# Row maxima transposed unclipped, with VectorE clipping, negating and flagging the transposed rows out of PSUM

## The chip, the cores and the metric

The kernel runs on one core of one Trainium2 chip. The metric is the device time of one execution in microseconds. Of the kernel before there are three timed runs, with a median of 907.64 us (907.53 to 913.1), and one profiled execution of 907.15 us, from which all rows below come.

## The reference, cut to what matters

Attention over 2 batches x 8 heads, 768 tokens, head size 64, in which a query sees only the keys whose nearest centroid (of 16) is its own; behind it two feed-forward networks on the 1536 x 512 result. What the change touches is the row maximum of the masked scores:

```python
scores = scale * np.matmul(q, k.transpose(0, 1, 3, 2))
scores = np.where(mask, scores, -1000000000.0)
scores = scores - np.max(scores, axis=-1, keepdims=True)
attn = np.exp(scores)
attn = attn / (np.sum(attn, axis=-1, keepdims=True) + 1e-09)
return np.matmul(attn, v).astype(np.float32)
```

A query whose cluster holds no key at all has every score at the same huge negative value. Its attention is then the mean of V, and the kernel treats it apart by a flag per query.

## The kernel before, in words

**Work and stages.** The 16 heads are taken as 8 pairs (`NP`). Behind a lead-in that fills the pipeline come 8 steps, `step(0)` to `step(7)`, then the two feed-forward networks. In step j three pairs are in work at once: pair j has its scores (`st`), exponentials (`et`) and products with V (`av`); pair j+1 (called m) has its row maxima; pair j+2 (p) has its transposes (`tp`), its products with the centroids (`dt`, `ds`) and its mask rows. POOL adds up the exponentials of a head over its key tiles (`ea`).

**Row maxima of pair m.** `maxes` (L278) computes for 128 queries and half the keys the masked scores again in PSUM (`mxs`, L283), and VectorE reduces each to a maximum (L289): 24 per step, kept in `mx`, 128 x 24. At the end of the step `max_rows1` (L293) reduces the two halves to one maximum per query and head, `mf`, 128 x 12 (L298). It then writes three blocks of 12 columns into `nm`: the maximum clipped from below and negated (L299), and twice the flag "no key" (L301). `max_rows2` (L304) transposes the 128 x 36 block on TensorE (`nt`, L309), ScalarE copies the rows into SBUF (`nr`, L311), and two moves that SP issues (both recorded at L138) carry them to where the next step's matmuls read them: row 80 of `QT` (read by every second score matmul, L352) and four flag rows of `GR` (read by the first matmul of `av`, L375, and by the sums, L397).

**What sets the order.** Each engine runs its instructions in the order in which they were written, and waits in place. The table `P` gives every piece of a step a position; the pieces are sorted by it. `max_rows1` stands at 21.65 and `max_rows2` at 26.91, so between the two stand, on TensorE, one or two matmul groups of `av` and nothing else. Behind the transpose on TensorE come the rest of `av`, the small V sum (`vt`, L327), the transposes of the next pair (`tp`, L164) and the first scores of the next step. SP carries all the moves and loads, in order. PSUM tiles that are named by `bank` rotate over six banks.

In the lead-in `max_rows1(0)` and `max_rows2(0)` run once, at a time at which POOL has no work. So there are eight of these transposes: one in the lead-in, seven at the ends of steps 0 to 6.

Of the kernel before, what the change touches and what calls it, by code (L numbers as in the profile page):

```python
# [10 lines left out]
F32 = mybir.dt.float32  # L11
F32R = mybir.dt.float32r
# [3 lines left out]
ALU = mybir.AluOpType  # L16
AX = mybir.AxisListType
BIG = float(2.0 ** 100)
CLIP = float(2.0 ** 60)
# [8 lines left out]
def clustered_attention_two_ffns(  # L28
# [20 lines left out]
    nc = tc.nc  # L49
    B, H, S, D = q.shape  # L50
    C = cent.shape[1]
    DM = out.shape[1]
    KF = w1.shape[0]
    NT = S // 128
# [10 lines left out]
    def bank(nm):  # L65
        nbank[0] += 1
        return ps1.tile([128, 512], F32, tag=f"s{nbank[0] % 6}", name=nm)
# [3 lines left out]
    ident = const.tile([128, 128], F32, name="ident")  # L71
# [14 lines left out]
    ap_ = att.enter_context(tc.tile_pool(name="att", bufs=1))  # L86
    et_p = att.enter_context(tc.tile_pool(name="et", bufs=6))
    ea_p = att.enter_context(tc.tile_pool(name="ea", bufs=2))
    nm_p = att.enter_context(tc.tile_pool(name="nmp", bufs=1))
# [4 lines left out]
    def slots(n, nm):  # L94
        last = (NP - 1) % n
        return [(ap_ if s == last else er2).tile([128, 2, 2, S], F32R, name=f"{nm}{s}") for s in range(n)]


    QT = slots(3, "qt")
# [7 lines left out]
    gv = ap_.tile([128, 128], F32R, name="gv")  # L107
    GR = [gr[64 * s:64 * s + 4] for s in range(2)]
    GV = [gv[64 * s:64 * s + 4] for s in range(2)]

    ok = set()
    qraw, kraw = {}, {}
# [24 lines left out]
    def move(dst, src):  # L137
        nc.sync.dma_start(out=dst.bitcast(F32), in_=src.bitcast(F32))  # L138
# [137 lines left out]
    nm_t = {}  # L276
# [11 lines left out]
            ok.add(("mx", j))  # L288
        nc.vector.tensor_reduce(out=nm_t[j][:, h, i, n:n + 1], in_=t[:, 0:HS], axis=AX.X, op=ALU.max)  # L289

    nr_t = {}

    def max_rows1(j):  # L293
        m = nm_t.pop(j)
        assert ("mx", j) in ok
        nm = nm_p.tile([128, 3, 2 * NT], F32, tag="nm", name="nm", bufs=2)
        mf = nm_p.tile([128, 2 * NT], F32, tag="mf", name="mf", bufs=2)
        nc.vector.tensor_reduce(out=mf, in_=m.rearrange("p h i n -> p (h i) n"), axis=AX.X, op=ALU.max)  # L298
        nc.vector.tensor_scalar(nm[:, 0, :], mf, -CLIP, -1.0, op0=ALU.max, op1=ALU.mult)  # L299
        for x in (1, 2):  # L300
            nc.vector.tensor_scalar(nm[:, x, :], mf, -CLIP, None, op0=ALU.is_le)  # L301
        nr_t[j] = nm

    def max_rows2(j):  # L304
        nm = nr_t.pop(j)
        assert j < 2 or ("sm", j - 2) in ok
        ok.add(("mr", j))
        t = bank("nt")
        nc.tensor.transpose(t[0:36, 0:128], nm.rearrange("p a b -> p (a b)"), ident)  # L309
        nr = nm_p.tile([36, 128], F32R, tag="nr", name="nr", bufs=2)  # L310
        nc.scalar.copy(nr, t[0:36, 0:128])  # L311
        move(QT[j % 3][64 + C:65 + C, 1, :, :], nr[0:12, :])
        move(GR[j % 2], nr[12:36, :])

    vs_t = {}

# [8 lines left out]
    def vsum2(j):  # L325
# [5 lines left out]
        tl = nm_p.tile([2, 128], F32R, tag="tl", name="tl")  # L331
        g = GV[j % 2]

# [34 lines left out]
    def av(j, kt, n):  # L368
# [4 lines left out]
        if kt == 0:  # L373
            assert ("gv", j) in ok
            nc.tensor.matmul(t[:, 0:HS], lhsT=GV[j % 2], rhs=GR[j % 2][:, r], start=True, stop=False)  # L375
        for h in range(2):
# [232 lines left out]
    with tc.manual_schedule():  # L609
# [27 lines left out]
        nc.gpsimd.memset(g768.bitcast(F32), 0.0)  # L637
        nc.gpsimd.memset(gr.bitcast(F32), 0.0)
        nc.gpsimd.memset(gv.bitcast(F32), 0.0)

# [7 lines left out]
        for _ in range(2):  # L650
            nc.vector.reciprocal(ss[:, 2:3], ss[:, 1:2])
            nc.vector.scalar_tensor_tensor(
                out=ss[:, 1:2], in0=ss[:, 2:3], scalar=ss[:, 0:1], in1=ss[:, 1:2], op0=ALU.mult, op1=ALU.add
# [26 lines left out]
        def step(j):  # L680
# [21 lines left out]
            put(at["V1"], lambda: vsum1(m), m is not None)  # L702
            put(at["V2"], lambda: vsum2(m), m is not None)
            put(at["MR"][0], lambda: max_rows1(m), m is not None)
            put(at["MR"][1], lambda: max_rows2(m), m is not None)
            put(at["LK"], lambda: late_k(m), m is not None)
            put(at["LD"], lambda: load(p + 1), p is not None and p + 1 < NP)
# [12 lines left out]
        lead += [(le["MV"][w], lambda w=w: moves(1, "qk"[w])) for w in range(2)]  # L720
        lead += [(le["V1"], lambda: vsum1(0)), (le["V2"], lambda: vsum2(0))]
        lead += [(le["MR"][0], lambda: max_rows1(0)), (le["MR"][1], lambda: max_rows2(0))]
        lead += [(le["MX"][x], lambda x=x: maxes(0, x)) for x in range(4 * NT)]
        for j in range(3):
# [24 lines left out]
        for c, fn in ((KF - 1, evac_av), (KF - 2, evac_sums)):  # L749
            t = pools["wb"].tile([128, 2 * NW], F32R, tag=f"w{c}", name="last").bitcast(F32)  # L750
# [79 lines left out]
```

## Time and profile before

| what | value |
|---|---|
| median of 3 runs | 907.64 us |
| profiled execution | 907.15 us |
| its span, first to last instruction | 905.4 us |
| PE busy | 838.6 us (93%) |
| DVE busy | 645.0 us (71%) |
| ACT busy | 442.0 us (49%) |
| POOL busy | 168.3 us (19%) |
| attention (lead-in and steps 0 to 7) | up to about 340 us |
| mean granted TensorE clock | 0.962 of full speed |

The span is what lies between the first and the last instruction; 1.75 us of the execution lie outside it. The steps repeat nearly to the microsecond: the maxima of step 4 are reduced at 221.56 us, those of step 5 at 259.34 us. So one step read closely stands for the others. Step 7 has no maxima of its own, and step 6 has no transposes of a next pair.

### The profile page before, as it was taken

The numbers are of one execution on the slowest core, as the hardware profiler recorded it, in microseconds if no ns is written. First come the engines' busy times: TensorE is split into PE (matmuls) and PEld (weight loads), VectorE is DVE, ScalarE is ACT, GpSimd is POOL, SyncE is SP. The second block draws the span as 40 slices with busy tenths as digits, with TensorE's granted clock in tenths as the row PEclk, the third lists the DMA queues.
The fourth block names the chain that finished last, engine by engine and source line by source line (L and its number), as shares of the span: only waits on it lengthen the run. The fifth ranks groups of instructions, "written<-read, shape, count | busy, mean of one in ns | idle before, by whom it ended". The sixth has DMA issues, their size and how long they took to land.

```text
span 905.4 us, 10141 instructions
## 1 busy us (share of the span) xinstructions
PE 838.6 (93%) x3721; PEld 612.2 (68%) x3721; DVE 645.0 (71%) x955; ACT 442.0 (49%) x772; POOL 168.3 (19%) x110
## 2 busy tenths in 40 slices
PE   6698898988989967999999999999899999999997
PEld 6565465654645425777888888876678878887885
DVE  6776877868768586887201137887999888888886
ACT  3145354553545534334322233335667776776764
POOL 2063745738458320000000000000000000000000
PEclk9598999999999979999999999999899999999999
DMA  9776364563620729000000005552000010001001
GB/s 195 172 162 146 62 140 89 116 145 77 141 54 12 303 86 401 0 1 1 1 0 1 1 23 209 186 186 93 1 1 1 0 47 1 1 0 47 1 1 47
DMA packets 44290, 71.37 MB, mean 79 GB/s; under 512 B 28320, under 2 KB 30672, under 8 KB 40144
## 3 DMA queue, kind: packets, MB, share of 16 engines
q1 hardware_dynamic: 44240, 70.72, 27.8%
q8 instruction: 29, 0.48, 0.2%
q14 instruction: 21, 0.17, 0.1%
HBM read 43.03 MB, written 3.15 MB: 51 GB/s over the span
## 4 chain that ended last, share of the span: by engine, by line
PE 57%; DVE 28%; ACT 10%; issue 3%; DMA 2%; SPq 0%; DVEq 0%; ACTq 0%
PE av L377 7%; PE h L513 6%; PE h L514 6%; PE h L515 6%; DVE w L474 4%; DVE w L480 4%; PE yp L589 4%; PE yp L590 4%; PE st L351 4%; PE yp L588 4%; PE mxs L283 3%; ACT w L484 3%; PE st L352 3%; DVE w L468 2%; PE yp L585 2%
## 5 line engine op out<-in xcount | busy, mean ns | idle before, releaser
L513 PE MATMUL h<-xh,w 128*128 128x512 f32 x384 | 151.1, 393 | 2.9 <-ACT last L410 2.9
L514 PE MATMUL h<-xl,w 128*128 128x512 f32 x384 | 150.9, 393 | 0.0
L515 PE MATMUL h<-xh,w 128*128 128x512 f32 x384 | 150.8, 393 | 0.0
L356 ACT ACTIVATE et<-st 128x384 f32<-128x384 f32 x192 | 88.6, 488 | 69.3 <-PE st L352 66.0
L289 DVE TENSOR_REDUCE mx<-mxs 128x1 f32<-128x384 f32 x192 | 98.1, 551 | 29.6 <-PE mxs L283 29.5
L362 POOL TENSOR_TENSOR ea<-ea,et 128x768 f32<-128x768 f32 x60 | 109.5, 1844 | 30.7 <-ACT et L356 30.7
L569 DVE TENSOR_TENSOR gl<-y,gh 128x512 fp32r<-128x512 f32 x48 | 33.2, 692 | 96.1 <-ACT gh L561 96.1
L377 PE MATMUL av<-et,vr 128*64 128x384 f32 x384 | 94.0, 565 | 5.8 <-ACT et L356 5.7
L484 ACT CAST w<-w 128x1024 fp32r<-128x1024 f32 x32 | 33.6, 1049 | 124.5 <-DVE w L480 124.5
L513 PEld LDWEIGHTS h<-xh,w 128*128 128x128 f32 x384 | 72.2, 188 | 20.0 <-ACT last L410 3.6
L515 PEld LDWEIGHTS h<-xh,w 128*128 128x128 f32 x384 | 72.2, 188 | 16.5
L514 PEld LDWEIGHTS h<-xl,w 128*128 128x128 f32 x384 | 72.2, 188 | 16.4
L588 PE MATMUL yp<-w,gh 128*128 128x512 f32 x192 | 76.9, 400 | 6.5 <-ACT gh L563 6.3
L585 PE MATMUL yp<-gl,w 128*128 128x512 f32 x192 | 77.6, 404 | 4.1 <-DVE gl L569 4.1
L584 PE MATMUL yp<-gh,w 128*128 128x512 f32 x192 | 76.8, 400 | 3.8 <-ACT gh L561 3.8
L589 PE MATMUL yp<-w,gl 128*128 128x512 f32 x192 | 77.5, 404 | 2.0 <-DVE gl L571 1.9
L590 PE MATMUL yp<-w,gh 128*128 128x512 f32 x192 | 76.3, 397 | 0.0
L586 PE MATMUL yp<-gh,w 128*128 128x512 f32 x192 | 75.5, 393 | 0.0
L351 PE MATMUL st<-qt,kk 128*128 128x384 f32 x192 | 73.6, 383 | 0.0
L526 ACT ACTIVATE y<-h 128x512 f32<-128x512 f32 x48 | 28.5, 594 | 81.9 <-PE h L515 81.8
L283 PE MATMUL mxs<-kt,qt 80*128 80x384 f32 x192 | 63.0, 386 | 5.6 <-DMA kt<-mr 5.6
L352 PE MATMUL st<-qt,kt 81*128 81x384 f32 x192 | 65.9, 343 | 0.0
(140 smaller groups left out, 1452.2 us busy)
## 6 DMA issues: line engine op xcount, KB each, us to landing
w<-in_moe_w SPq DMA_DIRECT2D x32, 1024.0 KB
qt<-hiq SPq DMA_DIRECT2D x16, 384.0 KB
kk<-hik SPq DMA_DIRECT2D x32, 192.0 KB
qraw<-in_q SPq DMA_DIRECT2D x8, 384.0 KB
kraw<-in_k SPq DMA_DIRECT2D x8, 384.0 KB
vr<-in_v SPq DMA_DIRECT2D x8, 384.0 KB
qt<-loq SPq DMA_DIRECT2D x16, 192.0 KB
kt<-hik SPq DMA_DIRECT2D x16, 192.0 KB
```

What stands on the lines that cost most here:

```text
L289: nc.vector.tensor_reduce(out=nm_t[j][:, h, i, n:n + 1], in_=t[:, 0:HS], axis=AX.X, op=ALU.max)
L351: nc.tensor.matmul(t[:, 0:HS], lhsT=KK[j % 2][:, h, c], rhs=QT[j % 3][:, 0, h, r], start=True, stop=False)
L352: nc.tensor.matmul(t[:, 0:HS], lhsT=KT[j % 3][0:65 + C, 1, h, c], rhs=QT[j % 3][0:65 + C, 1, h, r], start=False, stop=True)
L362: eng.tensor_tensor(out=ea[j, h], in0=et[j, 0, h] if first else ea[j, h], in1=e, op=ALU.add)
L377: nc.tensor.matmul(t[64 * h:64 * h + 64, 0:HS], lhsT=VR[j % 2][:, h, kt, :], rhs=et[j, kt, h][:, n, :], start=False, stop=kt == NT - 1,)
L513: nc.tensor.matmul(t, lhsT=wh[:, kk, :], rhs=h, start=kk == 0, stop=False)
L514: nc.tensor.matmul(t, lhsT=wh[:, kk, :], rhs=l, start=False, stop=False)
L515: nc.tensor.matmul(t, lhsT=wl[:, kk, :], rhs=h, start=False, stop=kk == KD - 1)
L585: nc.tensor.matmul(t, lhsT=wh[:, s], rhs=gl, start=False, stop=False)
L588: nc.tensor.matmul(t, lhsT=gh[:, s], rhs=wh, start=first, stop=False)
L589: nc.tensor.matmul(t, lhsT=gl[:, s], rhs=wh, start=False, stop=False)
L590: nc.tensor.matmul(t, lhsT=gh[:, s], rhs=wl, start=False, stop=last)
```

## The change

`max_rows1` now only reduces, and writes the unclipped maxima twice, 32 columns apart, into a tile `MF` that is zeroed once by POOL. `max_rows2` transposes 44 columns of that (12 maxima, 20 zeros, 12 maxima again). In place of ScalarE's copy, VectorE reads the transposed rows in PSUM: rows 0 to 11 are clipped and negated, rows 32 to 43 become flags, both written to `nr`. The flag rows go to `GR` by two moves of two rows each, where one move of four rows did it before.

```diff
+    MF = [ap_.tile([128, 2, 32], F32, name=f"mf{s}") for s in range(2)]
...
     def max_rows1(j):
-        m = nm_t.pop(j)
+        m = nm_t.pop(j).rearrange("p h i n -> p (h i) n")
         assert ("mx", j) in ok
-        nm = nm_p.tile([128, 3, 2 * NT], F32, tag="nm", name="nm", bufs=2)
-        mf = nm_p.tile([128, 2 * NT], F32, tag="mf", name="mf", bufs=2)
-        nc.vector.tensor_reduce(out=mf, in_=m.rearrange("p h i n -> p (h i) n"), axis=AX.X, op=ALU.max)
-        nc.vector.tensor_scalar(nm[:, 0, :], mf, -CLIP, -1.0, op0=ALU.max, op1=ALU.mult)
-        for x in (1, 2):
-            nc.vector.tensor_scalar(nm[:, x, :], mf, -CLIP, None, op0=ALU.is_le)
-        nr_t[j] = nm
+        nc.vector.tensor_reduce(
+            out=MF[j % 2][:, :, 0:2 * NT], in_=m.unsqueeze(1).to_broadcast([128, 2, 2 * NT, 2]), axis=AX.X, op=ALU.max
+        )
 
     def max_rows2(j):
-        nm = nr_t.pop(j)
...
-        nc.tensor.transpose(t[0:36, 0:128], nm.rearrange("p a b -> p (a b)"), ident)
-        nr = nm_p.tile([36, 128], F32R, tag="nr", name="nr", bufs=2)
-        nc.scalar.copy(nr, t[0:36, 0:128])
-        move(QT[j % 3][64 + C:65 + C, 1, :, :], nr[0:12, :])
-        move(GR[j % 2], nr[12:36, :])
+        w = 32 + 2 * NT
+        nc.tensor.transpose(t[0:w, 0:128], MF[j % 2].rearrange("p a b -> p (a b)")[:, 0:w], ident)
+        nr = nm_p.tile([w, 128], F32R, tag="nr", name="nr", bufs=2)
+        nc.vector.tensor_scalar(nr[0:2 * NT, :], t[0:2 * NT, 0:128], -CLIP, -1.0, op0=ALU.max, op1=ALU.mult)
+        nc.vector.tensor_scalar(nr[32:w, :], t[32:w, 0:128], -CLIP, None, op0=ALU.is_le)
+        move(QT[j % 3][64 + C:65 + C, 1, :, :], nr[0:2 * NT, :])
+        for x in range(2):
+            move(GR[j % 2][2 * x:2 * x + 2], nr[32:w, :])
...
+        for s in range(2):
+            nc.gpsimd.memset(MF[s], 0.0)
```

On VectorE, at the end of step 3, the order before was this (`mx` are the maxima, `t`, `gv` and `tl` the V sum, `loq` the next pair's queries):

```order
L289 TENSOR_REDUCE mx<-mxs 128x1 x13
L298 TENSOR_REDUCE mf<-mx 128x12
L299 TENSOR_SCALAR nm<-mf 128x12
L301 TENSOR_SCALAR nm<-mf 128x12 x2
L335 TENSOR_TENSOR t_1897<-vt,bm 2x128
```

It is now this, with line numbers of the changed kernel:

```order
L291 TENSOR_REDUCE mx<-mxs 128x1 x13
L297 TENSOR_REDUCE mf_112<-mx 128x2x12
L308 TENSOR_SCALAR nr<-nt 12x128
L309 TENSOR_SCALAR nr<-nt 12x128
L334 TENSOR_TENSOR t_1886<-vt,bm 2x128
```

Three small operations ahead of the transpose have become two behind it; all others keep their places. On TensorE the same place reads in the changed kernel as below; only the transposed width (36 before, 44 now) differs.

```order
L376 MATMUL av<-et,vr_109 64x384 x2
L306 MATMUL nt<-ident,mf_112 44x128
L376 MATMUL av<-et,vr_109 64x384 x2
L326 MATMUL vt<-vs,ones 2x128
L166 MATMUL tp<-ident,qraw 128x128 x6
L376 MATMUL av<-et,vr_109 64x384 x4
L166 MATMUL tp<-ident,kraw 128x128 x3
L350 MATMUL st<-qt_101,kk_106 128x384
```

On SP's queue the changed kernel has, at the same place, one move more:

```order
L130 DMA kraw<-in_k 128x12x64
L140 DMA qt_101<-nr 1x12x128
L140 DMA gr<-nr 2x6x128 x2
L140 DMA gv<-tl 2x128
L140 DMA qt_100<-hiq 64x2x768
```

Everything behind the `gr` moves stands one issue later than before. The copy of `nr` leaves ScalarE, eight times.

## Rows read from the trace of the kernel before

**Rows 1.** Waits of the whole span: engine, line, releaser: total us, times, longest us.

```profile
PE nt L309 <- DVE nm L301: 21.2, 8, 2.7
```

**Rows 2.** Instructions that write `nm`: durations in ns, first and last start in us.

```profile
L301 DVE TENSOR_SCALAR nm<-mf x16: 158/168/1773, 40.5 to 293.8; 128x12 f32<-128x12 f32 x16
```

**Rows 3.** Timeline of the end of step 4: start us, us, engine, line, instruction.

```profile
221.42 3.57 POOL L362 TENSOR_TENSOR ea<-ea,et 128x768 f32<-128x768 f32 x2 [1.21 <-ACT et L356]
...
221.56 0.87 PE L377 MATMUL av<-et,vr 128*64 128x384 f32 x4
221.56 0.18 DVE L298 TENSOR_REDUCE mf<-mx 128x12 f32<-128x24 f32 x1
221.77 1.48 DVE L299 TENSOR_SCALAR nm<-mf 128x12 f32<-128x12 f32 x1
223.17 1.85 DVE L301 TENSOR_SCALAR nm<-mf 128x12 f32<-128x12 f32 x2
...
225.07 0.29 PE L309 MATMUL nt<-ident,nm 128*36 128x128 f32 x1 [2.65 <-DVE nm L301]
...
225.29 1.37 PE L377 MATMUL av<-et,vr 128*64 128x384 f32 x4
...
225.68 0.86 SPq L138 DMA_DIRECT2D qt<-nr  x1
...
226.59 0.59 PE L327 MATMUL vt<-vs,ones 128*2 128x128 f32 x2
226.59 0.68 SPq L138 DMA_DIRECT2D gr<-nr  x1
...
227.11 1.54 PE L164 MATMUL tp<-ident,qraw 128*128 128x128 f32 x6
227.21 0.28 DVE L335 TENSOR_TENSOR t<-vt,bm 2x128 f32<-2x128 f32 x1 [2.20 <-PE vt L327]
...
228.57 1.20 DVE L176 SCALAR_TENSOR_TENSOR loq<-tp,hiq 128x384 fp32r<-128x384 f32 x2 [0.26 <-ACT hiq L173]
...
228.58 1.66 PE L377 MATMUL av<-et,vr 128*64 128x384 f32 x8
...
230.17 0.55 PE L164 MATMUL tp<-ident,kraw 128*128 128x128 f32 x3
...
230.47 0.42 PE L351 MATMUL st<-qt,kk 128*128 128x384 f32 x1
...
230.74 0.34 PE L352 MATMUL st<-qt,kt 81*128 81x384 f32 x1
...
234.46 0.43 PE L375 MATMUL av<-gr,gv 4*128 4x384 f32 x1
```

**Rows 4.** Timeline of the lead-in behind its transpose.

```profile
41.47 0.85 SPq L138 DMA_DIRECT2D qt<-nr  x1
...
43.83 0.52 PE L352 MATMUL st<-qt,kt 81*128 81x384 f32 x1
```

**Rows 5.** Stretches behind the seven waits: us, PE busy, granted clock, DMA share, GB/s.

```profile
72.25:79.10 6.85, 6.85 (x24) 0.53 0.18 37
111.52:117.02 5.50, 5.50 (x25) 0.69 0.17 37
...
225.07:230.47 5.40, 5.40 (x24) 0.68 0.01 4
262.84:267.18 4.34, 4.34 (x16) 0.61 0.02 4
295.61:300.79 5.18, 5.18 (x20) 0.67 0.16 32
```

**Rows 6.** Other stretches: us, then PE, PEld, DVE, ACT, POOL busy, clock, DMA share.

```profile
222.40:225.00 2.60, 0.02 (x2) 0.00 (x0) 2.60 (x3) 0.00 (x0) 2.59 (x2) 1.00 0.06 10
193.50:221.50 28.00, 27.16 (x145) 17.45 (x143) 23.27 (x39) 15.51 (x34) 18.23 (x12) 1.00 0.63 140
320.00:324.00 4.00, 1.48 (x4) 0.57 (x4) 2.89 (x3) 2.58 (x5) 1.07 (x1) 0.64 0.16 68
```

More of the change, by code (lines that the diff above doesn't have):

```diff
@@ L289, in maxes @@
         nc.vector.tensor_reduce(out=nm_t[j][:, h, i, n:n + 1], in_=t[:, 0:HS], axis=AX.X, op=ALU.max)
-    nr_t = {}
     def max_rows1(j):
-        m = nm_t.pop(j)
+        m = nm_t.pop(j).rearrange("p h i n -> p (h i) n")
         assert ("mx", j) in ok
-        nm = nm_p.tile([128, 3, 2 * NT], F32, tag="nm", name="nm", bufs=2)
-        mf = nm_p.tile([128, 2 * NT], F32, tag="mf", name="mf", bufs=2)
-        nc.vector.tensor_reduce(out=mf, in_=m.rearrange("p h i n -> p (h i) n"), axis=AX.X, op=ALU.max)
-        nc.vector.tensor_scalar(nm[:, 0, :], mf, -CLIP, -1.0, op0=ALU.max, op1=ALU.mult)
-        for x in (1, 2):
-            nc.vector.tensor_scalar(nm[:, x, :], mf, -CLIP, None, op0=ALU.is_le)
-        nr_t[j] = nm
+        nc.vector.tensor_reduce(
+            out=MF[j % 2][:, :, 0:2 * NT], in_=m.unsqueeze(1).to_broadcast([128, 2, 2 * NT, 2]), axis=AX.X, op=ALU.max
+        )
     def max_rows2(j):
-        nm = nr_t.pop(j)
         assert j < 2 or ("sm", j - 2) in ok
```

## The prediction

> **What bounds the kernel now.** I began with the list of waits, which adds up for each engine what it stood still for. TensorE is the busiest engine, so its waits are what can be won. Its largest is at the transpose of the row maxima, which waits for VectorE's small operations: 21.2 us in 8 waits [rows 1]. The longest, 2.7 us, is that of the lead-in; the other seven are 2.65 us each, 18.5 us together.
>
> Next, the durations of the operations waited for. The flag operation on 128x12 numbers takes 158 ns at the least and 1773 ns at the most [rows 2]: the same work, eleven times as long. The timeline of one step's end shows when [rows 3]. POOL runs two additions from 221.42 to 224.99, so one ends at about 223.2. VectorE's first small operation starts at 221.77 and lasts until 223.25; the next starts at 223.17, is drawn out to the end of POOL's second addition, and the third follows in no time. The reduction ahead of them, next to the same addition, took 0.18. So these operations stand still until POOL is done, and the reduction doesn't. TensorE is through with its products at 222.42 and stands until 225.07.
>
> The third view is the granted clock. In step 4's body, 28 us long, it is 1.00 [rows 6]. In each stretch that follows a wait it is between 0.53 and 0.69 [rows 5]: half speed for some microseconds after TensorE stood idle. The four products with V that took 0.87 before the wait take 1.37 behind it [rows 3]. So a wait costs more than its own length.
>
> **The change part by part.**
>
> *The wait of TensorE.* The transpose now needs only the reduction. That writes 24 numbers instead of 12; at 0.18 for twelve I give it at most twice that, until 221.92. TensorE arrives at 222.42, so it doesn't wait: 7 x 2.65 = 18.5 us less. What covers the reduction is the 0.87 us of products that TensorE runs beside it [rows 3]. In the lead-in POOL is idle, the operations cost some 0.17 each, and the wait there is for real work. I count nothing for it (up to 0.3 us).
>
> *The clock behind it.* In a stretch of length t at mean clock c, work that follows the clock would save t x (1 - c). For the five rows: 3.22, 1.71, 1.73, 1.69 and 1.71 [rows 5]; two more stretches, between the second and the third, are like these (5.43 and 5.41 us at 0.69 and 0.68). The sum is 13.5 us, the upper end. For a lower one I lay the instructions of the stretch at 225.07 at full pace [rows 3]: the transpose 0.22, four products 0.87, the V sum half its 0.52, six transposes 0.60 (three take 0.30 from 230.17 to 230.47), eight products 1.74, three transposes 0.30, together 3.99 of 5.40, so 1.41 saved against 1.73. That is 0.82 of it, or 11.0 us for all seven. I take the middle, 12.3.
>
> *The two operations behind the transpose.* VectorE clips and flags 12x128 numbers out of PSUM. No row shows this. The nearest is the small product with the V sum, which reads PSUM at 128 columns: 0.28 [rows 3]. Two make 0.56, in the place of one copy by ScalarE. From the transpose to the move it took 0.61 with the copy (225.07 to 225.68), so some 0.9 now. If POOL holds them as it held those before, each is held up to 1.8; that is a rival below. VectorE waits for the transpose from 221.92 to about 222.7, but what is queued behind it waits for TensorE anyway: the V sum's operations sat idle for 2.20 before they began [rows 3]. After them VectorE has 1.1 us of V sum (227.21 to 228.57 less 0.26 idle) and 1.20 of `loq`. From 222.7 that is 0.56 + 1.1 + 1.2, so 225.6 at best and some 226.2 with waits; the next step's scores come at about 222.42 + 3.85 = 226.3. It fits, narrowly. ScalarE's freed copy is worth nothing, since ScalarE waits there.
>
> *The moves.* The row for the scores leaves at 222.42 + 0.9 = 223.3. In the lead-in such a move was issued at 41.47 and its reader ran at 43.83 without a wait, so it lands within 2.36 us [rows 4]: by 225.7 here. Its reader follows the first score matmul by 0.27, at 226.5. Slack 0.8 us, where it was 2.7 by the same bound (225.68 + 2.36 against 230.74). The extra flag move costs SP about 0.7 us per step, 8 times; it stands ahead of the V sum's move and the next pair's queries, whose readers are microseconds or a step away. The second flag move goes out at about 224.9 and its reader, 3.99 us behind the first scores [rows 3], comes at 230.3. Nothing for the moves, then, and at worst some 0.3 us in step 5's and 6's end, which have fewer transposes to cover it. The next pair's raw queries, read 1.3 us after the wait's old start, have landed: DMA is nearly still from 222.4 on [rows 6].
>
> *The rest.* POOL's two additional memsets fall in the first microseconds. The body of a step keeps its order and its waits. At the hand-over to the networks TensorE is idle for most of the stretch from 320 to 324 while the DMA share is already down at 0.16 [rows 6], so it isn't the weights' transfer that holds it; the hand-over moves forward with the last step.
>
> The sum: 18.5 + 12.3 = 30.8 us off the profiled execution of 907.15, which is 876.4. The median of the runs stands 0.5 higher, so I predict **876.5**. The forecast's own span is 18.5 + 11.0 to 18.5 + 13.5 + 0.3 + about 3 us for what the trace doesn't order the same way twice: 872 to 881.
>
> **The rivals.**
>
> *POOL holds the new operations too.* They write SBUF while POOL's second addition runs until 224.99. Then the rows are ready at about 225.3 instead of 223.3, land by 227.7, and TensorE waits 1.1 to 1.2 us at the second score matmul in each of seven steps: 7 to 8 us back, 884. For: nothing in the trace reads PSUM in a tensor_scalar beside POOL. Against: what was held read SBUF alone, and the reduction beside the same addition wasn't held [rows 3]. Chance 0.10.
> The Trainium skill (VectorE: DVE Perf Modes, The perf-mode tier table) allows tensor_scalar up to twofold rate with a PSUM operand, which, if it came by a second port, would give this rival's 884; the same page's section on Mode 2×_2P says that PSUM has only one read port, which would give 876. No row of this trace decides between them.
>
> *The clock falls all the same.* The stretch behind the transpose is full of narrow products and transposes; if these, and not the wait, bring the clock down, only the wait is won: 907.15 - 18.5 = 888.6. For: this stretch is the only one that is slow. Against: it follows directly on the only long wait, in all seven places, and the body has short gaps (0.84 us in 28) at clock 1.00 [rows 6]. Chance 0.08.
>
> *The reduction is held.* Written twice from a repeated operand, it might be held where the old one wasn't. TensorE would resume at 223.3 instead of 222.42, which gives back 7 x 0.9 = 6 us and a part of the clock: 883 to 895. The change would then do half of what it says. Chance 0.03.
>
> *The gain is lost inside the steps.* VectorE's tail of 0.56 + 1.1 + 1.2 us reaches into the next step, whose PSUM tiles wait for its reductions; VectorE is busy for 23.27 of 28 us there [rows 6]. To bring the result within 1% (above 898) it would have to take back 22 of 31 us, 3 us per step. The body has 4.7 us per step in which VectorE could catch up. Chance 0.05, at about 903.
>
> *The flag rows become the wait, and the kernel slower.* SP now issues three moves where it issued two, and TensorE reaches the first product that reads the flags earlier. The second flag move has 230.3 - 224.9 = 5.4 us to land. Each us beyond is a wait in seven steps. The saving of 4.4 us per step is eaten from a landing time of 9.8 us on; at 12 us it would be 907 - 31 + 7 x 6.6 = 922. Against: 2.36 us bounds such a landing in the lead-in, with DMA busy [rows 4]. Chance 0.02.
>
> **How the numbers follow.** The forecast gets 0.72. Faster by over 1% (1% is about what a measurement here can tell from no change; it means under 898.5) are the forecast and the first three rivals: 0.72 + 0.10 + 0.08 + 0.03 = 0.93. Within 1% is the fourth, 0.05; slower the fifth, 0.02. A range from 872 to 888 holds the forecast, the held operations and the edge of the clock rival, a little over 0.8.
>
> **What would show it.** In the profile of the changed kernel the waits' list should have no row of the transpose waiting for VectorE but for the lead-in's; the granted clock between the transposes and the next scores should be 1.00, and a step should last 33.4 us where it lasted 37.8. The new operations should take about 0.28 each next to POOL; 1 us or more speaks for the first rival. Wrong would be a result above 888 with the wait gone: then the clock or a wait at the second score matmul has taken its place.

## The result and the profile after

The changed kernel took 877.84 us in the median of four runs (875.17 to 885.24), the kernel before, run beside it, 910.37 (907.53 to 917.9). The ratio is 0.965, with a 95% interval from 0.960 to 0.970: faster by 3.5%. This ratio and all below leave out, as slow, any run more than 1.5% above the fastest of its kernel. The profiled execution took 875.17 us, with a span of 873.4 us where it was 905.4, so 32.0 us less.

First the two kinds of instructions that the change brings in, grouped by the tile that they write (`nr`, the transposed rows; `mf`, the maxima ahead of the transpose). The columns are the duration in ns (least, median, most), the first and last start in us, and the shapes; the last line tells who waited for the tile, in us and times.

```profile
L308 DVE TENSOR_SCALAR nr<-nt x8: 278/279/280, 41.0 to 265.9; 12x128 fp32r<-12x128 f32 x8
L309 DVE TENSOR_SCALAR nr<-nt x8: 282/283/283, 41.3 to 266.2; 12x128 fp32r<-12x128 f32 x8
...
L297 DVE TENSOR_REDUCE mf<-mx x8: 203/204/204, 40.3 to 264.8; 128x24 f32<-128x48 f32 x8
...
  PE nt L306: 2.4, 1
```

Clipping and flagging out of PSUM take 0.28 us each, the longest no more than the shortest: none is held, though seven of the eight run beside POOL's additions. The flag operation of before went from 158 to 1773 ns [rows 2]. The reduction with twice the output takes 0.20. Of the eight waits of the transpose, 21.2 us [rows 1], one is left, that of the lead-in.

The timeline of a step's end, here step 1's, stands against that of before [rows 3] (start, duration in us, engine, line, instruction, idle time before and its releaser):

```profile
101.90 3.58 POOL L361 TENSOR_TENSOR ea<-ea,et 128x768 f32<-128x768 f32 x2 [1.21 <-ACT et L355]
102.04 0.20 DVE L297 TENSOR_REDUCE mf<-mx 128x24 f32<-128x48 f32 x1
...
102.04 0.87 PE L376 MATMUL av<-et,vr 128*64 128x384 f32 x4
...
102.84 0.29 PE L306 MATMUL nt<-ident,mf 128*44 128x128 f32 x1
...
103.06 0.87 PE L376 MATMUL av<-et,vr 128*64 128x384 f32 x4
103.17 0.28 DVE L308 TENSOR_SCALAR nr<-nt 12x128 fp32r<-12x128 f32 x1 [0.93 <-PE nt L306]
103.47 0.87 SPq L140 DMA_DIRECT2D qt<-nr  x1
103.48 0.28 DVE L309 TENSOR_SCALAR nr<-nt 12x128 fp32r<-12x128 f32 x1
...
104.59 0.97 DVE L335 CAST gv<-t 2x128 fp32r<-2x128 f32 x1
...
106.72 0.42 PE L350 MATMUL st<-qt,kk 128*128 128x384 f32 x1
```

POOL's two additions run as before, from 101.90 to 105.48. The transpose follows the products without a gap, and the four products behind it take 0.87 where they took 1.37. From the transpose to the next scores it is 3.88 us; before, it was 2.65 of standing still and 5.40 behind that [rows 3, 5]. A step, from one reduction `mf` to the next, takes 33.6 us where it took 37.8. One thing was not foreseen: the hold has moved on. The small cast of `gv` now falls beside POOL's second addition and takes 0.97. It takes 0.97 to 0.99 in all seven steps, and no matmul waits for it.

The stretches from the seven transposes to the scores stood at granted clocks from 0.53 to 0.69 before [rows 5]. Two of them and the last two now, the last one up to the fifth score matmul as in [rows 5] (stretch, us, PE busy, clock, DMA share, GB/s):

```profile
102.84:106.72 3.88, 3.88 (x27) 1.00 0.05 11
136.40:140.27 3.87, 3.87 (x26) 1.00 0.03 7
...
237.11:239.88 2.77, 2.77 (x18) 1.00 0.01 2
265.60:269.20 3.60, 3.60 (x22) 1.00 0.01 3
```

All seven are at 1.00. They became shorter by 2.97, 1.62, 1.56, 1.54, 1.53, 1.57 and 1.60 us, together 12.4. With 7 x 2.65 = 18.5 of waiting that makes 30.9 of the 32.0 us. Of the rest, 0.3 us lies ahead of the first of these step ends, 0.4 behind the last stretch, and 0.4 in small changes of the steps.

### The profile page after: what moved, and what is told of

It reads as the page before. It is cut to its first block, busy times and chain, and to the rows that moved or that the text cites. A ratio compares the mean times of both kernels' runs of the same rounds, so it can differ in the third digit from the quotient of the medians.

```text
span 873.4 us, 10161 instructions
## 1 busy us (share of the span) xinstructions
PE 825.5 (95%) x3721; PEld 607.1 (70%) x3721; DVE 631.2 (72%) x947; ACT 439.4 (50%) x764; POOL 168.5 (19%) x112
## 4 chain that ended last, share of the span: by engine, by line
PE 58%; DVE 25%; ACT 11%; issue 3%; DMA 2%; SPq 0%; DVEq 0%; ACTq 0%
PE av L376 7%; PE h L512 6%; PE h L513 6%; PE h L514 6%; DVE w L473 5%; DVE w L479 4%; PE st L350 4%; PE yp L588 4%; PE yp L589 4%; PE yp L587 4%; PE mxs L285 4%; ACT w L483 3%; PE st L351 3%; DVE w L467 2%; PE yp L584 2%
## 5 line engine op out<-in xcount | busy, mean ns | idle before, releaser
L483 ACT CAST w<-w 128x1024 fp32r<-128x1024 f32 x32 | 33.6, 1049 | 124.5 <-DVE w L479 124.5
L376 PE MATMUL av<-et,vr 128*64 128x384 f32 x384 | 86.8, 523 | 5.6 <-ACT et L355 5.5
```

The source lines that it names most:

```text
L376: nc.tensor.matmul(t[64 * h:64 * h + 64, 0:HS], lhsT=VR[j % 2][:, h, kt, :], rhs=et[j, kt, h][:, n, :], start=False, stop=kt == NT - 1,)
```

## The experiments

Two reasons stand behind the forecast: POOL's additions hold VectorE's small operations that read SBUF, and the standing still, not the narrow work behind it, brings the clock down. Each was tried from more than one side. Ratios are to the kernel before, run on the same chip.

**Only the source, in the kernel before.** The maxima go to PSUM; everything else stays as it was, three operations of 128x12 ahead of the transpose.

```
-        mf = nm_p.tile([128, 2 * NT], F32, tag="mf", name="mf", bufs=2)
+        t = bank("nt")
+        mf = t[:, 128:128 + 2 * NT]
```

> The kernel before with one thing altered: the reduced maxima lie in PSUM (in the bank that the transpose fills afterwards), so the three small operations ahead of the transpose read PSUM and not SBUF. Their number, order and place, ScalarE's copy and the two moves are those of before. Theory (operations that read SBUF stand still while POOL adds, those that read PSUM don't): each takes about 0.28 us, the transpose waits some 0.4 us in place of 2.65, the clock stays at 1.00; 907 - 7 x 2.25 - 12.4 = 879 us. Rival (what helps is that fewer operations stand ahead of the transpose, whatever they read): 907 us, wait of 2.65 as before.

Measured: median 876.56 (875.74, the profiled one, to 897.01), ratio 0.962 [0.954, 0.969]. The operations by tile, in the columns used above:

```profile
L302 DVE TENSOR_SCALAR nm<-nt x16: 159/160/161, 40.7 to 265.7; 128x12 f32<-128x12 f32 x16
L300 DVE TENSOR_SCALAR nm<-nt x8: 170/171/172, 40.6 to 265.5; 128x12 f32<-128x12 f32 x8
```

One operand moved from SBUF to PSUM takes the most from 1773 to 161 ns, with the writes still in SBUF and POOL's additions where they were. At 0.17 each the three are done inside the 0.87 us of products, so no wait is left in the steps at all. Of the changed kernel's parts, then, the one that matters is that VectorE reads PSUM; the clipping behind the transpose is one way to get there.

**Without POOL's last addition, in the kernel before.** The additions for the last key tile are left out for pairs 0 to 6, and with them a part of the sums.

```
-        if n == 1 and kt:
+        if n == 1 and kt and (kt < NT - 1 or j == NP - 1):
```

> The kernel before without POOL's additions of the last key tile of pairs 0 to 6 (the row sums then lack that tile's share). POOL is idle when VectorE runs the small operations at a step's end. Theory (POOL's additions hold them): 0.17 us each as in the lead-in, ready in 0.6 us beside 0.87 us of products, no wait; 907 - 18.5 - 12.4 = 876 us. Rival (the operations are slow at that place for another reason, such as their 12 columns or what ran before): still 1.5 to 1.8 us, 907 us.

Measured: 886.72 (profiled), 882.11, 875.95 and 891.76, ratio 0.968 [0.958, 0.977].

```profile
L301 DVE TENSOR_SCALAR nm<-mf x16: 165/166/168, 42.8 to 275.3; 128x12 f32<-128x12 f32 x16
```

With SBUF sources and POOL silent, none is held. With the run before it, that settles the first reason: it takes both, POOL's addition and a source in SBUF. The best run gives the forecast time; the others are up to 16 us above it, and the profile shows where a part of that is: four steps took 34.1 us and one 37.0, where a step of the changed kernel takes 33.6. Here are windows of 1 us behind the products with the centroids, which are 24 matmuls of 64 columns per step (L220):

```profile
88.00:89.00 1.00, 1.00 (x10) 0.96 1.08 212
89.00:90.00 1.00, 1.00 (x4) 0.50 1.03 203
90.00:91.00 1.00, 1.00 (x4) 0.50 1.04 243
91.00:92.00 1.00, 1.00 (x4) 0.50 1.01 240
92.00:93.00 1.00, 1.00 (x6) 0.84 0.40 101
93.00:94.00 1.00, 1.00 (x6) 1.00 0.02 6
```

The last of these products ends at 88.9 us. TensorE is busy all the time, and the clock falls to half. This was in neither theory; the last runs below go after it.

**The wait filled, in the kernel before.** Fourteen products of 384 columns, which nobody reads, go ahead of the transpose, so that TensorE works while VectorE is held.

```
+        if j:
+            for _ in range(FILL):
+                nc.tensor.matmul(t[:, 0:HS], lhsT=KK[(j - 1) % 2][:, 0, 0:128], ...
```

> The kernel before, in which TensorE runs 14 further matmuls of 384 columns (0.16 us each, 2.2 together, into the bank that the transpose then overwrites) at the place where it stood still at the ends of steps 0 to 6. VectorE's operations are held as before, so the transpose comes no earlier. Theory (the idle time brings the clock down): granted clock 1.00 behind the transposes, 12.4 us less, 895 us. Rival (the narrow products and transposes behind it bring the clock down): clock 0.5 there as before, 907 us.

Measured: median 895.06, ratio 0.983 [0.976, 0.989]; span 892.9, 12.5 less than before. The timeline of TensorE at step 4's end:

```profile
216.72 2.70 PE L312 MATMUL nt<-qt,kk 128*128 128x384 f32 x14
219.50 0.29 PE L315 MATMUL nt<-ident,nm 128*36 128x128 f32 x1
219.72 0.87 PE L383 MATMUL av<-et,vr 128*64 128x384 f32 x4
220.51 0.38 PE L333 MATMUL vt<-vs,ones 128*2 128x128 f32 x2
220.82 0.88 PE L165 MATMUL tp<-ident,qraw 128*128 128x128 f32 x6
221.63 1.51 PE L383 MATMUL av<-et,vr 128*64 128x384 f32 x8
```

The transpose comes as late as before, but behind it the four products take 0.87 and not 1.37, the eight 1.51 and not 1.66 [rows 3], at full pace. The same narrow work follows, and only the idle time is gone; so in these places the idle time was what brought the clock down. The seven stretches behind the transposes became 12.4 us shorter, as in the changed kernel: that is the clock's share by itself, beside the forecast 12.3. That the span gives nearly the same number is in part chance. From the end of step 0 to the end of the last stretch it is 11.9 us, since the transposes come a little later; the part ahead of that became 1.75 us longer and the part behind it 2.4 shorter.

**One held operation back in the path, in the changed kernel.** The clipping goes ahead of the transpose again, in SBUF; the flags stay behind it.

```
+        nc.vector.tensor_scalar(MF[j % 2][:, 0, 0:2 * NT], MF[j % 2][:, 1, 0:2 * NT],
+            -CLIP, -1.0, op0=ALU.max, op1=ALU.mult)
-        nc.vector.tensor_scalar(nr[0:2 * NT, :], t[0:2 * NT, 0:128], -CLIP, -1.0, ...
+        nc.scalar.copy(nr[0:2 * NT, :], t[0:2 * NT, 0:128])
```

> The changed kernel with one of the operations put back ahead of the transpose: VectorE clips and negates one copy of the maxima in SBUF, ScalarE copies these rows out of PSUM; the flags stay behind the transpose. Theory (one operation that reads SBUF is held to the end of POOL's first addition, some 1.5 us, of which 0.87 lies under TensorE's products): the transpose waits about 0.9 us in seven steps where it waited 2.65, 6 us more than the changed kernel: 881 to 882 us if 0.9 us of idle time leaves the clock at 1.00, 894 if the clock falls as before. Rival (only three operations in a row are held): 875 us.

Measured: 893.16 and 894.46, ratio 0.982 [0.975, 0.989]. The operation by tile, and, from the list of waits, the transpose's:

```profile
L300 DVE TENSOR_SCALAR mf<-mf x8: 173/1458/1467, 40.0 to 280.5; 128x12 f32<-128x12 f32 x8
...
  PE nt L309: 9.0, 8
```

The hold is back, 1.46 us, and the wait is as forecast: less the lead-in's 2.7, 6.3 us in seven, 0.9 each. A step of 33.6 became one of 34.5, with the clock at 1.00 behind the transpose. So 0.9 us of idle time there did not do what 2.65 did. The forecast for that case was 881 to 882; the total is some 10 us above it. It agrees with the 894 that was given for a clock that falls behind the wait, but in the profiled run the clock fell elsewhere: step 1 took 44.1 us, and of it

```profile
80.00:88.00 8.00, 8.00 (x45) 0.80 1.02 239
88.00:96.00 8.00, 8.00 (x25) 0.50 0.07 18
96.00:104.00 8.00, 8.00 (x25) 0.50 0.23 37
```

(windows of 8 us: PE busy, clock, DMA share, GB/s) two windows lie wholly at half speed, behind the centroid products, with TensorE fully busy.

**The rival's case made true, in the changed kernel.** ScalarE copies the transposed rows to SBUF, and VectorE clips and flags them from there, beside POOL.

```
+        ns = nm_p.tile([w, 128], F32, tag="ns", name="ns", bufs=2)
+        nc.scalar.copy(ns, t[0:w, 0:128])
-        nc.vector.tensor_scalar(nr[0:2 * NT, :], t[0:2 * NT, 0:128], ...
+        nc.vector.tensor_scalar(nr[0:2 * NT, :], ns[0:2 * NT, :], ...
```

(the flags likewise from `ns`)

> The changed kernel, but ScalarE first copies the transposed rows to SBUF and VectorE's two operations read them there. TensorE's transpose is as early as in the changed kernel. Theory: the first operation gets in between POOL's two additions, the second is held to the end of the second, 1.1 us later than in the changed kernel; the V sum and the next pair's low parts slide by as much and cost TensorE 0 to 0.8 us per step: 875 to 881 us, likeliest 878. Rival of the prediction (the held operations delay the score row): 883 to 885 us. If reading SBUF costs nothing here: 875 us and 0.2 us each.

Measured: 880.1, 876.6, 891.12 and 884.41, ratio 0.966 [0.955, 0.978].

```profile
L310 DVE TENSOR_SCALAR nr<-ns x8: 214/337/343, 42.4 to 270.8; 12x128 fp32r<-12x128 f32 x8
L311 DVE TENSOR_SCALAR nr<-ns x8: 217/1740/1744, 42.6 to 271.2; 12x128 fp32r<-12x128 f32 x8
```

POOL does hold what reads SBUF here too, but only the second operation in full. Behind the transpose the first meets the end of POOL's first addition and slips in before the next (0.34 us), so the row for the scores leaves in time, and the flags have time. Of steps 1 to 5 four take 33.6 us, as in the changed kernel; step 1 takes 37.1, with a fall of the clock right behind its centroid products. The rival's mechanism is real, and its price, 7 to 8 us, was not.

**One move instead of two, in the changed kernel.** A third copy of the maxima gives both flag rows in one operation of 24 rows, and one move takes them.

```
+        nc.vector.tensor_reduce(out=f[:, 32 + 2 * NT:32 + 4 * NT], in_=m, axis=AX.X, op=ALU.max)
-        for x in range(2):
-            move(GR[j % 2][2 * x:2 * x + 2], nr[32:w, :])
+        move(GR[j % 2], nr[32:w, :])
```

> The changed kernel with one flag move in place of two: the maxima are written a third time (one more reduction of 0.18 us), 56 columns are transposed, one operation of 24 rows makes the flags, and SP issues two moves per step as before the change. Theory (SP's extra issue of 0.7 us per step lies on no path): 875 us, within 0.5 of the changed kernel, fastest run against fastest. Rival (SP's third move delays what comes behind it): up to 7 x 0.7 = 5 us less, 870.

Measured: median 877.2 (874.98, the profiled one, to 898.02), ratio 0.963 [0.957, 0.969], span 873.2 beside 873.4. The extra move costs nothing, as forecast.

**The changed kernel as it is, once more.** What remains is the clock that falls with TensorE busy. First the same program again, six runs.

> The changed kernel as it is, beside the others on the same chip: fastest 875.2 us, single runs 5 to 10 us above it. If the clock theory holds, a profile of a run above 880 us shows stretches at 0.5 behind the centroid products, one of 875 none.

Measured: 875.89 to 890.74, median 879.13; the profiled one 880.13. Windows of 4 us of this execution, the same instructions in the same order as in the first profile of the changed kernel, which shows 1.00 at every one of these places:

```profile
84.00:88.00 4.00, 4.00 (x19) 0.64 1.05 213
...
116.00:120.00 4.00, 4.00 (x31) 0.91 1.04 223
120.00:124.00 4.00, 4.00 (x16) 0.66 0.77 185
152.00:156.00 4.00, 4.00 (x20) 0.68 1.05 217
156.00:160.00 4.00, 4.00 (x11) 0.50 0.31 77
160.00:164.00 4.00, 4.00 (x15) 0.54 0.00 0
```

Three steps took 34.1, 34.1 and 37.1 us where the others took 33.6: 0.5 + 0.5 + 3.5 = 4.5 us. So falls account for the profiled 880.13. That they make the slower runs slow isn't shown: the recorded mean clock of the run of 890.74 is 0.977 and that of 884.22 is 0.983, above the 0.974 of the fastest. Nor can these means rule it out, since the record misses stretches at half speed, as the next run shows. The kernel before spread as wide (907.53 to 917.9); its profiled run had no fall at these places.

**The centroid products moved.** Of the two groups of these products per step, the first goes 2.5 us earlier in the table that sets the order.

```
-    ... D=[7.73, 8.27], ...
+    ... D=[5.23, 8.27], ...
```

> The changed kernel with the first half of a step's centroid products (12 matmuls of 64 columns) moved from position 7.73 to 5.23, away from the second half at 8.27. In two of the profiles so far the clock fell to half right behind the 24 such matmuls, with TensorE busy all the time, at 3.5 us or so each, and single runs of the changed kernel took 5 and 10 us more than its fastest. Theory (that row of narrow matmuls brings the clock down in some executions): fewer or no such runs, median within 1 us of the fastest, 875. Rival (the runs differ for another reason, or each half alone does it): median 3 us or more above the fastest as for the changed kernel.

Measured: 885.03 to 901.56, median 893.42 (898.8 the profiled one), ratio 0.974 [0.968, 0.980], against 0.965 for the changed kernel. It mends nothing: a step takes 34.9 us, since TensorE now waits for VectorE's reduction of the products:

```profile
166.94 0.44 PE L350 MATMUL st<-qt,kk 128*128 128x384 f32 x1 [0.91 <-DVE ds L229]
```

Behind that wait the clock was at half from 169.0 to 182.6, and this step took 39.8 us. What the distance alone does is hidden by the new wait.

Another 10 us lie in step 0, which took 38.1 us where the changed kernel needs 28.1. A window of it (us, PE busy, clock, DMA share, GB/s), and two score matmuls from within:

```profile
60.00:64.00 4.00, 4.00 (x14) 1.00 0.00 0
...
61.80 0.53 PE L350 MATMUL st<-qt,kk 128*128 128x384 f32 x1
62.12 0.53 PE L351 MATMUL st<-qt,kt 81*128 81x384 f32 x1
```

The record says 1.00, but these matmuls start 0.32 us apart and last 0.53, where from 64 us on it is 0.18 and 0.34. TensorE ran at half pace until 63.1 us; in the changed kernel's first profile half pace ends at 44 us. So the record of the clock can miss a stretch, and a start that stays slow for long is a second candidate for the runs that are 10 us above the fastest.

**The centroid products halved, and doubled.** Halved leaves out the low part in steps 0 to 5 (12 matmuls per step instead of 24); doubled forms the same sums twice over in these steps (48), the second in place of the first.

```
-                for x in range(2):
+                parts = 1 if j > 1 else 2
+                for x in range(parts):
```

```
-                for x in range(2):
+                for x in (0, 1, 0, 1) if j > 1 else (0, 1):
```

> The changed kernel without the low-part half of the centroid products in steps 0 to 5: 12 narrow matmuls per step in place of 24 (their result is then less exact). By their pace of 0.11 us it takes 6 x 1.33 = 8 us out by itself: 867 us. Theory (24 narrow matmuls in a row let the clock fall in some executions): no stretch at 0.5 in the body of the steps, runs within 2 us of each other. Rival (the falls hang on something else): runs spread over 10 us as those of the changed kernel did (875.9 to 890.7).

> The changed kernel with the centroid products of steps 0 to 5 run twice into the same place: 48 narrow matmuls per step, same result. By the pace of 0.11 us that adds 6 x 2.67 = 16 us by itself: 891 us. Theory: the clock falls behind them in all six steps, at 0.5 to 3.5 us each as in the profiles so far: 894 to 912 us, stretches at 0.5 in each step. Rival: 891 us in the fastest run and a fall in some steps only.

Measured, halved: 873.24 to 884.29, median 874.55, ratio 0.962 [0.956, 0.967]. By the signs that were set the theory failed here: the clock still fell in three steps of the profiled run, and the runs spread over 11 us. Each fall cost 0.4 us (34.0 beside 33.6). All three begin some 4.5 us behind the narrow products, and 1.6 to 1.9 behind a wait of almost 1 us for VectorE's reduction; but the same waits in steps 1 and 2 were not followed by a fall. So this run doesn't separate the two causes. The 12 matmuls left out saved 1.3 us in step 0 and nothing in the undisturbed steps 1 and 2, 33.6 as before, because TensorE waits for VectorE there. TensorE's waits in step 1 of the halved kernel:

```profile
85.17 0.44 PE L351 MATMUL st<-qt,kk 128*128 128x384 f32 x1 [0.97 <-DVE ds L230]
90.14 0.35 PE L263 MATMUL ot<-ident,ds 128*64 128x128 bf16 x3 [0.94 <-DVE ds L252]
```

The first of the two is new, and the second was there before (0.85 in the changed kernel). The expectation had counted the whole length of what was left out.

Doubled: median 937.31, ratio 1.023 [1.015, 1.031], far above what was expected. Five of the steps have a fall in the records, each 7 to 24 us long, and step 0 took 46.5 us, at half pace until 75.9 us with 1.00 in the record. Windows of one of them:

```profile
178.00:180.00 2.00, 2.00 (x16) 1.00 0.98 290
180.00:184.00 4.00, 4.00 (x28) 0.74 1.05 210
184.00:188.00 4.00, 4.00 (x20) 0.50 0.54 134
188.00:192.00 4.00, 4.00 (x13) 0.50 0.00 0
196.00:200.00 4.00, 4.00 (x15) 0.50 0.02 4
204.00:206.00 2.00, 2.00 (x7) 0.54 0.05 9
206.00:208.00 2.00, 2.00 (x13) 1.00 0.60 137
```

TensorE is busy without a gap, falls to half speed among the narrow products (179.2 to 187.6 us) and stays there for some 24 us. In this one profile, then, more of these products came with more and longer falls. That they cause them is a reading and not shown: halving them did not end the falls, and why one execution has three and another none stays open.

## Why the prediction was right

*The wait.* Right, in place, in cause and in size: 18.5 us. The cause was read from two lines in one timeline, small operations that end when POOL's additions end, beside a reduction that doesn't [rows 3]. The runs with a PSUM source and without POOL's addition show it from both sides.

*The clock.* Right: 12.3 forecast, 12.4 measured, in the changed kernel and with the wait filled. That the middle between the two bounds, 13.5 and 11.0, came out so closely is luck; no row spoke for the middle.

*The total.* The two terms give 30.9 of the 32.0 us that the span lost; the other 1.1 had no term. The number itself has a slip: 876.4 for the profiled execution and 0.5 more for the median make 876.9, not 876.5. The median of 877.84 lies 1.3 us from the first and 0.9 from the second; with runs of one kernel 10 us apart, a hit that close is in part luck.

*The new operations.* Right: 0.28 each, taken from a product that reads PSUM at 128 columns. The move leaves 0.63 us behind the transpose, not 0.9, since the row for the scores needs only the first of them. The Trainium skill (VectorE: DVE Perf Modes, Mode 2×_2P) says that PSUM has only one read port; a hold-free 0.28 beside POOL, and 0.16 at 12 columns, agree with it and not with the rival's reading, that a PSUM operand might come by a second port.

*What was costed at nothing.* The moves (one fewer changes the span by 0.2 us), the reduction (0.20, inside the products' 0.87) and the hand-over cost nothing, as forecast. VectorE's tail did become longer by a hold that the sum didn't have: the cast of `gv`, 0.97 in place of 0.22. `loq` is done at 107.05, 0.33 us after the next scores begin, later than the forecast "narrowly", and still TensorE doesn't wait. The forecast could have had it: a small operation with an SBUF source was seen to be held next to POOL [rows 3], and with the first ones gone from there, others come into that place.

*The rivals.* That POOL holds the new operations was false; the run that makes it true shows that it would have cost nothing in a step without a fall, because two operations behind POOL's two additions are not both held in full. The rival that narrow work brings the clock down was false where it was put: behind the transposes it is the idle time. Elsewhere it may hold: behind the 24 narrow products of a step the clock falls in some executions with TensorE busy, which cost 0.5 to 3.5 us at a time in the changed kernel. The forecast had no term for it; the trace of before shows 1.00 at those places. It explains the profiled 880.13, but why runs of the changed kernel reach from 875 to 891 stays open, as a long start at half pace costs 10 us too. Of the other three rivals nothing came: the reduction took 0.20, TensorE has no new wait inside the steps, and no matmul waited for a flag row.

*No better version.* The kernel before with its maxima in PSUM (ratio 0.962) and the one with a single flag move (0.963) lie inside the changed kernel's interval. The halved products have a lower median (874.55), but their ratio (0.962) lies inside it too, and they leave work out.

## What to carry to other kernels

When a small VectorE operation has a least and a most duration far apart, look at what POOL runs beside the long ones, and try the operand in PSUM before reordering anything: here moving one small tile in the kernel before gave the whole gain. Price a wait of TensorE by its length and by the slower clock behind it, here two thirds as much again for waits of 2.65 us (12.4 on 18.5), and nothing beyond their length for waits of 0.9 us in the same place. And before a gain of under 1% is believed or doubted, look whether the clock of both profiled executions is 1.00 in the same places, and whether the same matmul takes the same time there, since the record of the clock can miss a stretch.

## What was not expected of the hardware

- The hold goes by addition, not by operation: with two additions of 1.8 us back to back, VectorE gets one operation in between them. The first operation lasts to the end of the addition that it meets (1.46 us, or 0.34 when it starts late), the next to the end of the following one (1.74).
- Where TensorE stood still for 2.65 us ahead of the transposes, the clock fell to half within the next microseconds, in all seven steps. 0.9 us in the same place did not bring it down (34.5 us per step, clock 1.00), and 0.9 to 1.0 us in the middle of a step was followed by a fall in some steps (the moved and the halved products) and by none in others.
- The clock also falls while TensorE shows 100% busy, behind or among groups of matmuls of 64 columns: from 1.00 to 0.50 at 89 us in the kernel without POOL's last addition, for some 3 us; for about 10 us in the changed kernel's second profile; for some 24 us with the groups doubled. Which execution has it could not be told from the order of the instructions, which was the same.
- The recorded clock can read 1.00 while TensorE runs at half pace: up to 63.1 us with the centroid products moved (matmuls of 384 columns 0.32 us apart, later 0.18) and up to 75.9 with them doubled.
